# Two weight tiles on a second DMA queue, their high halves on the vector engine, and the first chunk's products in three passes

## The chip, the core and the metric

The kernel runs on one core of a Trainium2 chip. A core has five engines with an instruction queue each: TensorE (PE, the matrix products), VectorE (DVE), ScalarE (ACT), GpSimd (POOL) and SyncE (SP, which here only issues DMA transfers). The engines run side by side and wait for each other through semaphores. The metric is the device time of one execution in microseconds, lower is better.

## The reference, cut to what matters

```python
def reference(A_x, A_wqkv, A_wo, B_x, B_w1, B_b1, B_w2, gate_w):
    x = A_x                                          # (1, 2048, 640); B_x is not used
    g = sigmoid((x * gate_w).sum(-1, keepdims=True))
    a = A_ref(x, A_wqkv, A_wo)     # qkv = x @ wqkv; 32 heads of 20; softmax over 8 keys at distance 0, 2, ..., 14; @ wo
    b = B_ref(x, B_w1, B_b1, B_w2) # h = x @ w1 + b1 (640 -> 1728); h * tanh(softplus(h)); @ w2 (1728 -> 640)
    return g * a + (1 - g) * b
```

All of it is float32. Only the first product, x @ wqkv, is touched by the change, and of it only the first part.

## The kernel before

**Three products for one.** TensorE works on a rounded format (float32r). So every float32 operand is split into a high half (a copy into the rounded format) and a low half (operand minus high half), and every product is made of three: high x high, high x low, low x high (`mm3`, lines 347 to 351: L349, L350, L351). `split` (L312) makes the halves: the high one by ScalarE (L314), the low one by the vector engine, or by whichever of VectorE and GpSimd is free (L317). `load_pair` (L335) puts a load (`dma`, L322, issued by SP at L323) and a split together.

**Tiling.** The 640 input features are five chunks of 128 (`kc` 0 to 4). The 2,048 positions are four blocks of 512 (`tb`); a tile of x is one block and one chunk, 128 x 512. The tiles of wqkv, `WQ[hq, kc]`, are 128 x 498 for the first group of heads: q, k and v of eight heads, some columns of w1, and gate_w twice. They are named x0 to x4 and w0 to w4 here for `tb` 0 and `hq` 0, by chunk.

**The start.** Nine products of zeros warm TensorE up (L291). Then the first unit of `qkv` (L456, the case `u == 0`) goes chunk by chunk over four output banks, as the tiles come in: for every chunk four times `mm3`, 12 products. Bank i takes positions 128 i to 128 i + 127 of the block as its stationary operand, the weight tile is the moving one. The other four banks follow, each with all its chunks, and then the products of the first dense layer, `mlp1`. The attention of a unit (`attention`, L381) is the vector engine's, and begins when its q, k and v are out of the banks.

**What sets the order.** The program is written as a list of tasks (`add`, L74) with an engine, a duration, a rank, what they come after, and the buffers that they take. `Plan.run` (L90) plays them on a clock of its own and so fixes the order of the instructions in each engine's queue. It looks at the engines in the order PE, ACT, DVE, POOL, SP (`LAG`, L62); a free engine takes, of its tasks that are ready and whose buffers are free, the one of the lowest rank, then the earliest in the list. Buffers come from rings, and a task may take one only in the order in which they were asked for (`fits`, L105). The staging buffers of the loads go round three rings, three to each (`stages`, L325): x0 and w0 take the first two of `raw`; x1, w1 and x2 those of `hb`; w2, x3 and w3 those of `e`; x4 and w4 are on `raw` again. A task's result counts as there for tasks of other engines after a lag of 120 ns (ACT, DVE) or 1,900 ns (SP, behind the transfer itself), for tasks of its own engine after 40 ns. What the chip does with the order, it does by semaphores; the planner's clock is not the chip's.

The activation tables are loaded at L254, ahead of everything that is planned.

Of the kernel before, what the change touches and what calls it, by code (L numbers as in the profile page):

```python
# [59 lines left out]
class Plan:  # L60
# [29 lines left out]
    def run(self):  # L90
        ready = {e: [] for e in self.LAG}
        busy = dict.fromkeys(self.LAG, False)
        events, n, left, wire = [], 0, len(self.tasks), 0.0


        quiet, gate, last, shared, phase, begun = 0.0, None, None, [], "", False
        loud = sum(t.kind != "" for t in self.tasks)
        for i, t in enumerate(self.tasks):
            t.key = (t.rank, i)
            t.rdy = 0.0  # L100
            if not t.waits:
                (shared if t.both else ready[t.eng]).append(t)
        now = 0.0

        def fits(t):  # L105
            want = {}
            for b in t.take:
                want[b.ring] = want.get(b.ring, 0) + 1
                if b.ring.free < want[b.ring] or b.ring.line[b.ring.at + want[b.ring] - 1] is not b:
                    return False  # L110
            return True

        while left:
            again = True
            while again:
                again = False
                for e in self.LAG:
                    if busy[e]:
                        continue
                    fit = [t for t in ready[e] if fits(t)]  # L120
                    on = begun and loud
                    if e == "POOL":
                        fit += [t for t in shared if fits(t)]
                        if on:
                            fit = [t for t in fit if now + t.ns[0] <= quiet + 150 or t.rank < 0]
                    elif e == "DVE":
                        fit += [t for t in shared if fits(t) and (now - t.rdy > self.PATIENCE or phase != "qk" or not on)]
                    if not fit:
                        continue
                    t = min(fit, key=lambda t: t.key)  # L130
                    if t.both:
                        shared.remove(t)
                        t.eng = e
                    else:
                        ready[e].remove(t)
                    if type(t.ns) is tuple:
                        t.ns = t.ns[e == "DVE"]
                    for b in t.take:
                        b.ring.free -= 1
                        b.ring.at += 1  # L140
                        b.t = b.make()
                    t.start = now
                    ins = t.fn(e) if t.both else t.fn()
                    if e == "POOL" and on and quiet > now and gate and ins:
                        self.follow(ins, gate)
                    if e == "DVE":
                        if t.kind:
                            begun = True
                            loud -= 1
                            phase = t.kind[:2]  # L150
                        if t.kind == "qk":
                            quiet, gate = now + 5700, last
                        last = ins or last
                    busy[e] = again = True
                    heapq.heappush(events, (now + t.ns, n, "idle", e))
                    end = now + t.ns
                    if e == "SP":
                        wire = max(wire, end) + t.land
                        end = wire
                    heapq.heappush(events, (end + self.LAG[e], n + 1, "done", t))  # L160
                    if e != "SP":
                        heapq.heappush(events, (end + 40, n + 2, "own", t))
                    n += 3
            if not events:
                stuck = [(t.eng, t.rank, t.waits, getattr(t.fn, "__qualname__", "")) for e in ready for t in ready[e]]
                raise RuntimeError(f"nothing can go on at {now}, {left} left: {stuck[:20]}")
            now, _, what, x = heapq.heappop(events)
            if what == "idle":
                busy[x] = False
                continue  # L170
            if what == "done":
                left -= 1
                x.at = now
                for b in x.hold:
                    b.left -= 1
                    if not b.left:
                        b.ring.free += 1
            for t in x.then:

                if (t.eng == x.eng and x.eng != "SP") != (what == "own"):  # L180
                    continue
                t.waits -= 1
                if not t.waits:
                    t.why, t.rdy = x, now
                    (shared if t.both else ready[t.eng]).append(t)
        return now
# [3 lines left out]
def kernel(ctx: ExitStack, tc: tile.TileContext, x, wq, wo, w1, b1, w2, out):  # L190
# [42 lines left out]
    def act_ns(n):  # L233
        return 95 + 0.95 * n
# [10 lines left out]
    def mm_ns(n):  # L245
        return 13.5 + (n + 15) // 16 * 16 / 2.4
# [4 lines left out]

    A.preload_act_table_set("natural_log_exp_and_others")  # L254
    bias = keep.tile([128, FC + 1], F32)
    ln2 = keep.tile([128, 1], F32)
    cap = keep.tile([128, 1], F32)
# [51 lines left out]
    cg = add("POOL", 5000, consts_g, rank=-1)  # L309


    def split(raw, hi, lo, n, after, eng, hold, take=(), rank=SOON):  # L312

        a = add("ACT", act_ns(n), lambda: A.activation(hi(), raw(), AF.Copy), after, rank=rank, take=take, hold=hold)  # L314

        def low(e=eng):
            return (V if e == "DVE" else G).tensor_tensor(lo(), raw(), hi().bitcast(F32), op=OP.subtract)  # L317

        b = add(eng, either(eng, n), low, [a], rank=rank, hold=list(take) + list(hold))
        return [a, b]  # L320

    def dma(out_ap, in_ap, after=(), rank=0.0, take=(), hold=(), size=262144):  # L322
        return add("SP", 450, lambda: nc.sync.dma_start(out_ap(), in_ap()), after, rank=rank, take=take, hold=hold, size=size)  # L323

    stages = {"i": 0, "of": (raw_buf, raw_buf, raw_buf, lambda: h_buf("hb"), lambda: h_buf("hb"), lambda: h_buf("hb"),  # L325
# [6 lines left out]
        stages["i"] += 1  # L332
        return stages["of"][stages["i"] % len(stages["of"])]()

    def load_pair(src, eng, n=512, rank=SOON, drank=0.0, after=(), wide=False, home=None):  # L335
        raw, p = stage(wide), pair_buf() if home is None else fixed(home)
        d = dma(lambda: raw.t[:, :n], src, after, rank=drank, take=[raw], size=n * 512)
        p.ready = split(lambda: raw.t[:, :n], lambda: p.t[:, 0, :n], lambda: p.t[:, 1, :n], n, [d], eng, [raw], [p], rank)
        return p

    def load_w(src, n, eng, rank=NEXT, drank=0.0, after=()):
# [94 lines left out]
    def qkv_part(ps, P, hq, i, kc, n):  # L436
        xs = tuple(X[2 * P + i // 4, kc].t[:, j, (i % 4) * 128:(i % 4 + 1) * 128] for j in range(2))
        mm3(ps.t[:, :n], xs, tuple(WQ[hq, kc].t[:, j, :n] for j in range(2)), kc == 0, kc == KC - 1)

    def qkv_evac(u, P, hq, i, ps, done):  # L440
        kv, q, s = KV[UNIT[u]], Q[UNIT[u]], 4 * (1 - i // 4) + i % 4
        before = freed.get((u - 2, s), []) if u < 7 else [zero2[0]]
        a = add("ACT", 400, lambda: A.activation(kv[:, 7 + s], ps.t[:, QF:3 * QF].rearrange("p (a b) -> p a b", a=2), AF.Copy),  # L443
                [done] + before, rank=SOON, hold=[ps])
        b = add("ACT", 280, lambda: A.activation(q[:, s], ps.t[:, :QF], AF.Copy), [a], rank=SOON, hold=[ps])

        def rest():
            A.activation(hx[:, P, i, hq], ps.t[:, 3 * QF:3 * QF + RQ], AF.Copy)
            if hq == 0:
                z = ps.t[:, NCOL - 2:NCOL - 1]  # L450
                A.activation(zt[:, P, s:s + 1], z, AF.Exp, scale=-1.0)

        c = add("ACT", 170 * (2 if hq == 0 else 1), rest, [b], rank=SOON, hold=[ps])
        return a, b, c

    def qkv(u, P, hq):  # L456
# [3 lines left out]
        pss = [ps_buf() for _ in range(8)]  # L460
        if u == 0:
            last = warmed
            for kc in range(KC):
                for i in range(4):
                    last = pe_add(3 * mm_ns(n), lambda i=i, kc=kc: qkv_part(pss[i], P, hq, i, kc, n),
                               [last] + X[0, kc].ready + WQ[hq, kc].ready, take=[pss[i]] if kc == 0 else [],
                               hold=[pss[i], X[0, kc], WQ[hq, kc]])
                    if kc == KC - 1:
                        ev[i] = qkv_evac(u, P, hq, i, pss[i], last)
# [232 lines left out]
    def wq_in(hq, kc, eng, **k):  # L702
        n = NCOL if hq == 0 else NCOL - 2
        WQ[hq, kc] = load_pair(lambda: wq[hq, kc][:, :n], eng, n=n, wide=hq == 0, **k)
# [3 lines left out]

    for kc in range(KC):
        x_in(0, kc, "DVE", drank=-1.0)  # L710
        wq_in(0, kc, "DVE", drank=-1.0)
    bias_in = dma(lambda: bias, lambda: b1, rank=-0.5, size=7168)
    const_v = add("DVE", 400, consts_v, [bias_in], rank=NEXT)
    for kc in range(KC):
# [93 lines left out]
```

## Time and profile before

| What | Value |
|---|---|
| median of 3 runs | 657.4 us (657.2 to 657.87) |
| the profiled execution's own time | 657.01 us |
| its span, first to last instruction | 655.2 us |
| mean granted TensorE clock | 0.999 |
| TensorE busy | 648.8 us |
| VectorE busy | 558.7 us |
| ScalarE busy | 349.9 us |
| GpSimd busy | 61.6 us |

In a row of the timeline stand start and duration in us, the engine, the line of the kernel, the operation, the tile written and the tile read, and in brackets the idle time of the engine ahead of it and what ended it. SPq is SP's queue of DMA issues; the duration there is that of the issue and not of the transfer. A row of a view by stretch gives from and to, the length, then busy us and number of instructions for PE, PEld (weight loads of TensorE), DVE, ACT and POOL, then the granted TensorE clock, the share of time that the DMA engines were busy, and GB/s. A row of a view of DMA issues gives the tiles, the count, the size, and the us from issue to landing. Tiles of x for the first block go to a fixed place and are called kvq after their split; weight tiles are called pair.

### The profile page before, as it was taken

Reading aid. Unit: us, or ns where it says so; the run is one execution under the profiler, and the core shown is the slowest. Engines: PE = TensorE matmul, PEld = TensorE weight load, DVE = VectorE, ACT = ScalarE, POOL = GpSimd, SP = SyncE. Lnnn points to the kernel's source line nnn. Section 1 sums busy time; section 2 is a strip of 40 time slices with the busy share of each in tenths; the row PEclk is TensorE's granted clock in tenths of the full one; section 3 lists DMA queues with packets and bytes.
Section 4 is the critical chain, followed back from the end, with each engine's and each line's share of the span. In section 5 each row is a group of like instructions: output and inputs, shape, how many; then the busy total and the mean of one; then the engine's idle time right before and its main releaser. Section 6 shows DMA issues by size and latency. Waiting matters only on the chain.

```text
span 655.2 us, 8076 instructions
## 1 busy us (share of the span) xinstructions
PE 648.8 (99%) x2869; PEld 537.6 (82%) x2869; DVE 558.7 (85%) x495; ACT 349.9 (53%) x724; POOL 61.6 (9%) x41
## 2 busy tenths in 40 slices
PE   9999999999999999999999999999999999999997
PEld 6888888888888888888888887888888888888886
DVE  6599999999998998999899989999999999934311
ACT  6689469639928963982896275434423134313100
POOL 2121000000000000000100100036002400212000
PEclk9999999999999999999999999999999999999999
DMA  9763355322314431331234267825546226645322
GB/s 312 235 49 113 99 112 120 111 64 84 106 57 139 126 106 33 89 121 57 77 106 145 58 186 243 263 66 168 166 116 200 78 75 202 186 130 159 114 80 81
DMA packets 55017, 82.38 MB, mean 126 GB/s; under 512 B 8144, under 2 KB 23760, under 8 KB 54976
## 3 DMA queue, kind: packets, MB, share of 16 engines
q1 hardware_dynamic: 54976, 81.86, 42.6%
q8 instruction: 22, 0.36, 0.2%
q14 instruction: 19, 0.16, 0.1%
HBM read 44.94 MB, written 27.80 MB: 111 GB/s over the span
## 4 chain that ended last, share of the span: by engine, by line
PE 98%; DVE 1%; issue 0%; DMA 0%; ACT 0%; SPq 0%; DVEq 0%
PE bank L350 32%; PE bank L351 32%; PE bank L349 32%; PE bank L614 1%; PE bank L615 1%; DMA raw<-in_wq 0%; DVE pair L317 0%; DVE kvq L693 0%; ACT pair L314 0%; DVE pr L407 0%; SPq L323 0%; DVEq L317 0%
## 5 line engine op out<-in xcount | busy, mean ns | idle before, releaser
L350 PE MATMUL bank<-pair 128*128 128x512 f32 (+2 forms) x432 | 167.3, 387 | 1.3 <-DVE pair L317 1.3
L349 PE MATMUL bank<-pair 128*128 128x512 f32 (+2 forms) x432 | 167.0, 387 | 0.0
L351 PE MATMUL bank<-pair 128*128 128x512 f32 (+2 forms) x432 | 167.0, 387 | 0.0
L386 DVE TENSOR_TENSOR pr<-kvq 128x2560 f32<-128x2560 f32 x32 | 92.4, 2887 | 4.6 <-issue 4.1
L350 PEld LDWEIGHTS bank<-pair 128*128 128x128 f32 x432 | 81.1, 188 | 17.7 <-DVE pair L317 2.2
L349 PEld LDWEIGHTS bank<-pair 128*128 128x128 f32 x432 | 81.1, 188 | 16.5 <-ACT kvq L638 0.6
L351 PEld LDWEIGHTS bank<-pair 128*128 128x128 f32 x432 | 81.2, 188 | 15.5
L350 PE MATMUL bank<-pair,w 128*128 128x512 f32 x234 | 91.0, 389 | 0.0
L349 PE MATMUL bank<-pair,w 128*128 128x512 f32 x234 | 91.0, 389 | 0.0
L351 PE MATMUL bank<-pair,w 128*128 128x512 f32 x234 | 91.0, 389 | 0.0
L407 DVE TENSOR_TENSOR pr<-kvq,lg 128x2560 f32<-128x2560 f32 x32 | 90.1, 2817 | 0.7
L389 DVE TENSOR_REDUCE lg<-pr 128x128 f32<-128x2560 f32 x32 | 90.0, 2812 | 0.5
L443 ACT ACTIVATE kvq<-bank 128x320 f32<-128x320 f32 x64 | 27.9, 439 | 97.1 <-PE bank L351 96.5
L350 PE MATMUL bank<-pair,kvq 128*128 128x512 f32 (+2 forms) x196 | 75.8, 387 | 0.2 <-DVE pair L317 0.2
L351 PE MATMUL bank<-pair,kvq 128*128 128x512 f32 (+2 forms) x196 | 75.9, 387 | 0.0
L349 PE MATMUL bank<-pair,kvq 128*128 128x512 f32 (+2 forms) x196 | 75.8, 387 | 0.0
L349 PEld LDWEIGHTS bank<-pair,w 128*128 128x128 f32 x234 | 43.9, 188 | 9.2
L351 PEld LDWEIGHTS bank<-pair,w 128*128 128x128 f32 x234 | 43.9, 188 | 9.2
L350 PEld LDWEIGHTS bank<-pair,w 128*128 128x128 f32 x234 | 43.9, 188 | 9.1
L411 DVE TENSOR_TENSOR pr<-pr 128x1280 f32<-128x1280 f32 x32 | 48.8, 1525 | 0.3
L525 DVE SCALAR_TENSOR_TENSOR hb<-e,hb 128x512 f32<-128x512 f32 (+1 forms) x56 | 39.7, 710 | 10.3 <-ACT e L523 10.0
L314 ACT ACTIVATE pair<-raw 128x512 fp32r<-128x512 f32 (+2 forms) x53 | 32.9, 628 | 27.7 <-PE bank L351 16.9
(94 smaller groups left out, 893.4 us busy)
## 6 DMA issues: line engine op xcount, KB each, us to landing
act<-hb SPq DMA_DIRECT2D x52, 256.0 KB, 2.0
o<-ot SPq DMA_DIRECT2D x64, 80.0 KB, 1.9
raw<-act SPq DMA_DIRECT2D x20, 256.0 KB, 3.5
raw<-in_w SPq DMA_DIRECT2D x15, 320.0 KB, 3.0
kvq<-kvq SPq DMA_DIRECT2D x8, 560.0 KB, 4.1
e<-act SPq DMA_DIRECT2D x17, 256.0 KB, 2.8
hb<-act SPq DMA_DIRECT2D x15, 256.0 KB, 3.1
raw<-in_wq SPq DMA_DIRECT2D x15, 248.0 KB, 3.7
```

Source lines behind the costliest of these rows:

```text
L314: a = add("ACT", act_ns(n), lambda: A.activation(hi(), raw(), AF.Copy), after, rank=rank, take=take, hold=hold)
L349: nc.tensor.matmul(ps, ah, bh, start=first, stop=False)
L350: nc.tensor.matmul(ps, ah, bl, start=False, stop=False)
L351: nc.tensor.matmul(ps, al, bh, start=False, stop=last)
L386: return V.tensor_tensor(pr, window(kv, s0, 0), q[:, s0:s0 + 2, None, :].to_broadcast([128, 2, W, QF]), op=OP.mult)
L389: V.tensor_reduce(lg[:, s0:s0 + 2].rearrange("p s w h -> p (s w h)"), pr.rearrange("p s w (h d) -> p (s w h) d", d=DH), op=OP.add, axis=AX.X)
L407: V.tensor_tensor(pr.rearrange("p s w (h d) -> p s w h d", d=DH), vw, lg[:, s0:s0 + 2, :, :, None].to_broadcast([128, 2, W, HQ, DH]), op=O ...
L411: prev = add("DVE", 1510, lambda: V.tensor_tensor(pr[:, :, 0:4], pr[:, :, 0:4], pr[:, :, 4:8], op=OP.add), [prev], rank=r)
L443: a = add("ACT", 400, lambda: A.activation(kv[:, 7 + s], ps.t[:, QF:3 * QF].rearrange("p (a b) -> p a b", a=2), AF.Copy), [done] + before, ...
L525: v = add("DVE", 700, lambda: V.scalar_tensor_tensor(hb.t[:n], e.t[:n], -1.0, hb.t[:n], op0=OP.add, op1=OP.mult), [a], rank=NEXT, hold=[e, ...
L614: nc.tensor.matmul(pss[dc].t, wh, p.t[:, 0], start=False, stop=False)
L615: nc.tensor.matmul(pss[dc].t, wl, p.t[:, 0], start=False, stop=True)
```

## The change

Four things change. The loads of w0 and w1 become tasks of ACT's queue instead of SP's, with rank -3; the planner lets a transfer that is not SP's land 1,900 ns plus its size by 270 bytes per ns after its issue. The high halves of w0 and w1 become copies by the vector engine. The table load moves from ahead of the plan into it, as a task of ACT of rank -2. And chunk 0 of the first unit goes by pass over the four banks, high x high for all four, then high x low, then low x high, each pass a task that waits for its own halves, instead of bank by bank.

```diff
@@ -157,6 +157,8 @@
                     if e == "SP":
                         wire = max(wire, end) + t.land
                         end = wire
+                    else:
+                        end += t.land
                     heapq.heappush(events, (end + self.LAG[e], n + 1, "done", t))
@@ -251,7 +253,6 @@
-    A.preload_act_table_set("natural_log_exp_and_others")
     bias = keep.tile([128, FC + 1], F32)
@@ -309,9 +310,12 @@
-    def split(raw, hi, lo, n, after, eng, hold, take=(), rank=SOON):
-
-        a = add("ACT", act_ns(n), lambda: A.activation(hi(), raw(), AF.Copy), after, rank=rank, take=take, hold=hold)
+    def split(raw, hi, lo, n, after, eng, hold, take=(), rank=SOON, hi_eng="ACT"):
+
+        if hi_eng == "DVE":
+            a = add("DVE", 400, lambda: V.tensor_copy(hi(), raw()), after, rank=rank, take=take, hold=hold)
+        else:
+            a = add("ACT", act_ns(n), lambda: A.activation(hi(), raw(), AF.Copy), after, rank=rank, take=take, hold=hold)
@@ -319,7 +323,10 @@
-    def dma(out_ap, in_ap, after=(), rank=0.0, take=(), hold=(), size=262144):
+    def dma(out_ap, in_ap, after=(), rank=0.0, take=(), hold=(), size=262144, eng="SP"):
+        if eng == "ACT":
+
+            return add("ACT", 450, lambda: A.dma_start(out_ap(), in_ap()), after, rank=rank, take=take, hold=hold, size=1900 * 270 + size)
         return add("SP", 450, lambda: nc.sync.dma_start(out_ap(), in_ap()), after, rank=rank, take=take, hold=hold, size=size)
@@ -437,6 +444,12 @@
+    def qkv_pass(pss, a, b, n):
+
+        for i, ps in enumerate(pss):
+            nc.tensor.matmul(ps.t[:, :n], X[0, 0].t[:, a, i * 128:(i + 1) * 128], WQ[0, 0].t[:, b, :n],
+                             start=a == b, stop=False)
+
@@ -460,10 +473,15 @@
             last = warmed
-            for kc in range(KC):
+            xh, xl = X[0, 0].ready
+            wh, wl = WQ[0, 0].ready
+            for a, b, w in ((0, 0, [xh, wh]), (0, 1, [wl]), (1, 0, [xl])):
+                last = pe_add(4 * mm_ns(n), lambda a=a, b=b: qkv_pass(pss[:4], a, b, n), [last] + w, take=pss[:4] if a == b else [],
+                              hold=pss[:4] + [X[0, 0], WQ[0, 0]])
+            for kc in range(1, KC):
                 for i in range(4):
                     last = pe_add(3 * mm_ns(n), lambda i=i, kc=kc: qkv_part(pss[i], P, hq, i, kc, n),
-                               [last] + X[0, kc].ready + WQ[hq, kc].ready, take=[pss[i]] if kc == 0 else [],
+                               [last] + X[0, kc].ready + WQ[hq, kc].ready,
                                hold=[pss[i], X[0, kc], WQ[hq, kc]])
@@ -708,7 +726,9 @@
     for kc in range(KC):
         x_in(0, kc, "DVE", drank=-1.0)
-        wq_in(0, kc, "DVE", drank=-1.0)
+        wq_in(0, kc, "DVE", drank=-1.0 if kc > 1 else -3.0, **({"queue": "ACT", "hi_eng": "DVE"} if kc < 2 else {}))
+        if kc == 1:
+            add("ACT", 1300, lambda: A.preload_act_table_set("natural_log_exp_and_others"), rank=-2.0)
```

`load_pair` passes `queue` and `hi_eng` on to `dma` and `split`.

More of the change, by code (lines that the diff above doesn't have):

```diff
@@ L333, in stage, with load_pair @@
         return stages["of"][stages["i"] % len(stages["of"])]()
-    def load_pair(src, eng, n=512, rank=SOON, drank=0.0, after=(), wide=False, home=None):
+    def load_pair(src, eng, n=512, rank=SOON, drank=0.0, after=(), wide=False, home=None, queue="SP", hi_eng="ACT"):
         raw, p = stage(wide), pair_buf() if home is None else fixed(home)
-        d = dma(lambda: raw.t[:, :n], src, after, rank=drank, take=[raw], size=n * 512)
-        p.ready = split(lambda: raw.t[:, :n], lambda: p.t[:, 0, :n], lambda: p.t[:, 1, :n], n, [d], eng, [raw], [p], rank)
+        d = dma(lambda: raw.t[:, :n], src, after, rank=drank, take=[raw], size=n * 512, eng=queue)
+        p.ready = split(lambda: raw.t[:, :n], lambda: p.t[:, 0, :n], lambda: p.t[:, 1, :n], n, [d], eng, [raw], [p], rank, hi_eng)
         return p
```

## The prediction

> **What bounds the kernel now.** I read the page first: busy shares, then the chain that ended last.
>
> ```profile
> PE 648.8 (99%) x2869; PEld 537.6 (82%) x2869; DVE 558.7 (85%) x495; ACT 349.9 (53%) x724; POOL 61.6 (9%) x41
> PE 98%; DVE 1%; issue 0%; DMA 0%; ACT 0%; SPq 0%; DVEq 0%
> ```
>
> TensorE is busy for 648.8 of 655.2 us and carries 98% of the chain. So only its idle time can be won, and any idle time added to it is paid in full. Where the idle time lies is read from busy time by stretch (first PE figure: busy us).
>
> ```profile
> 82.00:164.00 82.00, 82.00 (x367) 68.57 (x366) 77.03 (x66) 59.20 (x121) 1.58 (x1) 1.00 0.40 98
> 164.00:400.00 236.00, 236.00 (x1061) 198.60 (x1060) 221.37 (x175) 158.22 (x344) 6.26 (x5) 1.00 0.35 106
> 400.00:410.00 10.00, 8.71 (x37) 6.50 (x36) 9.90 (x13) 6.18 (x11) 0.00 (x0) 1.00 0.74 214
> 410.00:650.00 240.00, 240.00 (x1060) 198.25 (x1059) 182.72 (x177) 67.88 (x113) 40.40 (x23) 1.00 0.46 139
> ```
>
> From 82 to 650 us TensorE stands still once, for 10.00 - 8.71 = 1.29 us near 403. The change works on the first 9 us. There the timeline of before (start, duration, engine, line) is, for the first tiles of x (x0, x1) and of the weights (w0, w1):
>
> ```profile
> 0.75 1.28 ACT L254 ACT_TABLE_LOAD   x1 [0.75 <-PEq L796]
> 0.75 0.38 SPq L323 DMA_DIRECT2D raw<-in_x  x1
> 0.87 0.27 DVE L287 MEMSET lg<- 128x256 uint32 x1 [0.87 <-PEq L796]
> 1.19 0.42 SPq L323 DMA_DIRECT2D raw<-in_wq  x1
> 1.20 3.93 PE L291 MATMUL bank<-lg 128*128 128x512 bf16 x9 [1.20 <-DVE lg L287]
> 1.65 0.43 SPq L323 DMA_DIRECT2D hb<-in_x  x1
> 3.52 0.63 ACT L314 ACTIVATE kvq<-raw 128x512 fp32r<-128x512 f32 x1 [1.49 <-DMA raw<-in_x]
> 4.18 0.69 DVE L317 TENSOR_TENSOR kvq<-raw,kvq 128x512 fp32r<-128x512 f32 x1 [3.04 <-ACT kvq L314]
> 4.20 0.62 ACT L314 ACTIVATE pair<-raw 128x498 fp32r<-128x498 f32 x1
> 4.86 0.68 DVE L317 TENSOR_TENSOR pair<-raw,pair 128x498 fp32r<-128x498 f32 x1
> 4.88 0.49 PE L349 MATMUL bank<-pair,kvq 128*128 128x498 f32 x1
> 5.59 0.49 PE L350 MATMUL bank<-pair,kvq 128*128 128x498 f32 x1 [0.22 <-DVE pair L317]
> 6.24 0.63 ACT L314 ACTIVATE kvq<-hb 128x512 fp32r<-128x512 f32 x1 [1.42 <-DMA hb<-in_x]
> 6.90 0.69 DVE L317 TENSOR_TENSOR kvq<-hb,kvq 128x512 fp32r<-128x512 f32 x1 [1.37 <-ACT kvq L314]
> 7.55 0.68 DVE L317 TENSOR_TENSOR pair<-hb,pair 128x498 fp32r<-128x498 f32 x1
> 7.96 0.39 PE L351 MATMUL bank<-pair,kvq 128*128 128x498 f32 x1
> 8.19 0.38 PE L349 MATMUL bank<-pair,kvq 128*128 128x498 f32 x1
> ```
>
> The first real product starts at 4.88, when w0's high half is there; the second waits for w0's low half (4.86 + 0.68 = 5.54) until 5.59; the second chunk starts at 8.19. From 5.59 to 8.19 lie the 11 other products of chunk 0, 2.60 us, and the last two starts are 0.23 apart.
>
> The landings, issue to last byte (last column, us):
>
> ```profile
> raw<-in_x SPq DMA_DIRECT2D x1, 256.0 KB, 2.7
> raw<-in_wq SPq DMA_DIRECT2D x1, 249.0 KB, 3.0
> hb<-in_x SPq DMA_DIRECT2D x1, 256.0 KB, 4.6
> hb<-in_wq SPq DMA_DIRECT2D x1, 249.0 KB, 4.8
> ```
>
> The SP queue's issues stand about 0.47 apart (1.19, 1.65), so w1 goes out near 2.12. x0 lands at 3.5, w0 at 4.2, x1 at 6.2, w1 at 6.9. ScalarE stood idle for x1 until 6.24. So the transfers do not land at an even pace: x1 comes 2.0 us behind w0, w1 0.7 behind x1.
>
> **The change part by part.** *The issues.* The planner walks its engines in the order PE, ACT, DVE, POOL, SP, and a load may start only when its staging buffer is next in its ring. At time 0 the raw ring's next buffer belongs to x0, which SP has not taken yet, and the hb ring's to x1. So neither weight load fits, and ACT takes the only task that does: the table load, whatever the ranks say. ACT's queue becomes table load, w0, w1; SP's becomes x0, x1, w2, x3, x2, w3, x4. The planner's clock is used here for order alone.
>
> When ACT's queue gets to w0 no row shows: it is bounded by the start of the load (0.75) and the first thing ACT is seen to do after it (3.52). Before, w0 went out at 1.19. I take the load's end, 0.75 + 1.28 = 2.03, the row in between. The two issues (0.42 to 0.43 each on SP) end by 2.9, inside ACT's idle 1.49 us before 3.52, so they cost nothing; were that cover gone, x0's high half would be late by as much. SP loses two issues, so x1 goes out at 1.19, in w0's old place.
>
> *The landing of x1, L.* Low end: w0's old landing, 4.20. High end: x1's row, 6.24. Between them lies x0's 3.52 plus two transfers at 0.68 (6.24 to 6.92), 4.88. The same three transfers, x0, x1 and w0, have to come through before x1 and w0 are both complete, and in the trace the third came at 6.24; so I go nearer to that row and take L = 5.7, for w0 likewise.
>
> The Trainium skill, "DMA: Bandwidth & Descriptors" (section "Issuing engines are not separate DMA queues"), says that transfers issued from different engines run on the same 16 DMA engines and interleave, and that several issuers save only issue time. This speaks against the change, and by it w0 gains nothing from a queue of its own; by "a second queue is a second path" w0 and x1 would both be in by 4.9. No run of before has two queues, so the trace does not decide.
>
> *The vector engine.* It now makes w0's and w1's high halves. A copy of that shape is in no row: at least 0.27 (a memset of half as many elements), at most 0.69 (two inputs, same size); I take 0.5, twice the memset. By the planner's own figures it runs x0's low half to 4710 ns, w0's high half from 4714 to 5114, and then w0's low half becomes eligible at 5154, while x1's low half has been so since 4993. So x1's low half goes in first. The order is x0 low, w0 high, x1 low, w0 low, w1 high, w2 low, w1 low. That is the wait the change adds: w0's low half, which every product of the second pass needs, stands behind x1's landing, x1's high half on ScalarE and x1's low half.
>
> Priced with the rows of before: from ScalarE's start on x1 (6.24) to the end of the second low half (7.55 + 0.68 = 8.23) pass 1.99 us. So w0's low half ends at L + 1.99, against 5.54 before. w0's high half (5.7 + 0.5 = 6.2) is done before x1's low half may start (5.7 + 0.66), so it costs nothing; a landing of w0 over 0.16 us after x1's would show.
>
> *Pass by pass.* The same 12 products, each with its own weight load as before. The four high-high ones run while the low half is awaited, three more than before: 3 x 0.23 = 0.69 us won. After w0's low half come 8 products: 2.60 - 0.69 = 1.91. Chunk 1 starts at L + 1.99 + 0.05 + 1.91 = L + 3.95, against 8.19: the delay is L - 4.24. With L = 5.7: +1.5 us. With 6.24: +2.0. With 4.88: +0.6. With 4.20 the vector engine binds instead: x0 low until 4.87, w0 high until 5.37, then 0.65 (6.90 to 7.55) and 0.68, so 6.70, and 6.70 - 5.54 - 0.69 = +0.5. No value of L makes it a gain.
>
> *What comes next.* w1's low half ends 0.5 + 0.65 + 0.68 = 1.8 us after w0's; TensorE wants it 0.05 + 1.91 + 0.23 = 2.2 after, so it is just covered, if w2 is in. Two ScalarE copies go (0.62 each), the vector engine gains two of 0.5: hidden in its waits (3.04, 1.37). x2 goes out behind x3, and w4 behind three loads that it led; each is wanted by its own chunk, one every 2.7 us (12 x 0.23) from 8.19 on: x2 at 10.9, w4 at 16.4. w4's row of before:
>
> ```profile
> 6.96 0.33 SPq L323 DMA_DIRECT2D raw<-in_wq  x1
> raw<-in_wq SPq DMA_DIRECT2D x1, 249.0 KB, 4.7
> ```
>
> It landed at 11.7, so three loads of 0.7 to 0.9 us ahead of it are covered by 4.7 us. x2 lands as the seventh transfer, about 3 us after x1; its low half ends well before chunk 2, which is late by the same delay.
>
> *To the end.* The first attention follows TensorE:
>
> ```profile
> 33.40 2.83 DVE L386 TENSOR_TENSOR pr<-kvq 128x2560 f32<-128x2560 f32 x1 [4.10 <-issue]
> ```
>
> The vector engine idles 4.10 us before it, so it starts later by the same amount, and TensorE has no idle time until 403 that could take up a delay. In the planner's books chunk 1 begins 0.14 us earlier than before, a uniform shift once the first loads are used up, so I expect the later order to stay.
>
> Sum: the profiled run took 657.01 us (span 655.2); +1.5 gives 658.5. The median of the runs shown is 657.4, so 658.9.
>
> **The rivals.** *1, the queues help (not slower).* ACT's queue passes the table load at once and the slow landing of x1 was SP's backlog: L between 4.2 and 4.9, +0.5 to +0.65, about 658.0, no measurable change. For it: the later transfers land 0.7 apart. Against it: x1's row, 6.24. It decides below L = 5.5, where the delay is under 1.3.
>
> *2, the table load holds ACT's queue.* w0 goes out near 3.4 and lands 3.0 to 4.6 later (both rows above), at 7.2 in the middle; high half to 7.7, x1 low 0.65, low half 0.68, so 9.0: 9.0 - 5.54 - 0.69 = +2.8, 660.2. For it: no ACT row between 2.03 and 3.52.
> The Trainium skill, "ScalarE: Activation LUTs" (section "What ACT_TABLE_LOAD costs"), adds to about 1283 ns of load some 1380 ns of drain. The load's row agrees (1.28); no row shows the drain.
>
> *3, the clock falls.* The granted clock (third column from the right) at the end of the trace:
>
> ```profile
> 650.00:653.40 3.40, 1.47 (x7) 0.89 (x5) 1.37 (x2) 0.00 (x0) 0.00 (x0) 1.00 0.30 111
> 653.50:655.20 1.70, 0.00 (x0) 0.00 (x0) 0.00 (x0) 0.00 (x0) 0.00 (x0) 0.50 0.17 64
> ```
>
> After 3.4 us with 1.47 busy it is half. Between the warm-up's end (5.13) and 7.7 TensorE would now do four products, about 1.2 us; a stretch of 3.4 us around that holds 1.2 + 0.8 = 2.0, not far off. Half the clock for 3.4 us costs 1.7: 657.4 + 1.5 + 1.7 = 660.6.
> The Trainium skill, "TensorE: Matmul & The Clock Gate" (Part 1), has the clock gated again after an idle window of about 3.4 us; the two rows agree, and by it gaps of 1.2 us each are too short.
>
> *4, the planned order shifts later on*, and with it the stall at 403:
>
> ```profile
> 403.52 0.50 PE L350 MATMUL bank<-pair 128*128 128x512 f32 x1 [1.08 <-DVE pair L317]
> 407.46 0.50 PE L350 MATMUL bank<-pair 128*128 128x512 f32 x1 [0.20 <-DVE pair L317]
> ```
>
> TensorE waits there for low halves queued behind attention steps. If they go first it saves up to 1.3: 657.6, and less with a small L; one more step of 2.83 ahead of them would cost that much. Against it: the uniform shift.
>
> **How the numbers follow.** What tells from no change here is about 0.2%, 1.3 us. Forecast 0.47, of which 0.12 with L under 5.5 stays inside that bound; rival 1 0.17; rival 2 0.10; rival 3 0.14; rival 4 0.12 (0.05 faster, 0.04 same, 0.03 slower). Slower 0.35 + 0.10 + 0.14 + 0.03 = 0.62, same 0.12 + 0.17 + 0.04 = 0.33, faster 0.05. The likeliest case's own range is 658.2 (L 5.0) to 659.4 (6.24). The whole range, 657.7 to 660.6, takes in rivals 1 and 2 and reaches to 3.
>
> **What would show it.** Right: on ACT the table load ahead of two issues; on the vector engine x1's low half ahead of w0's; four high-high products, a wait for a low half, then eight; chunk 1 starting 0.6 to 2.0 later than 8.19; the same shift at 33.40 and at the end. Wrong: w0's low half before 6.2, products over 0.4 us apart after 8, or another stall than the one near 403.

## The result, and the profile after

| What | Before | After |
|---|---|---|
| median of 20 executions each | 657.22 us | 657.95 us |
| lowest and highest | 656.84 to 657.87 | 657.66 to 659.6 |
| the profiled execution's own time | 657.01 us | 659.59 us |
| its span | 655.2 us | 657.8 us |

The ratio is 1.0015, with a 95% interval of 1.0009 to 1.0022. The kernel became slower, by 0.7 us of median (0.6 to 1.4 by the interval). That is real, but inside the 0.2%, 1.3 us, that the prediction took as the bound of "no change".

The 20 executions of the change fall into two groups: 16 lie at 657.66 to 658.64, four at 659.19 to 659.6. The profiled execution belongs to the upper group, so its 2.58 us over before have to be taken apart into what the change always costs and what only some executions pay.

The start comes first. In the timeline of the changed kernel, the rows of before have these counterparts (L316 is the vector engine's copy, L318 ScalarE's, L321 the low half, L450 the product by passes, L356 to L358 the three products of `mm3`):

```profile
0.74 1.28 ACT L731 ACT_TABLE_LOAD   x1 [0.74 <-PEq L816]
...
0.77 0.39 ACTq L329 DMA_DIRECT2D raw<-in_wq  x1
1.19 0.42 SPq L330 DMA_DIRECT2D hb<-in_x  x1
1.19 0.46 ACTq L329 DMA_DIRECT2D hb<-in_wq  x1
...
4.99 0.51 DVE L316 CAST pair<-raw 128x498 fp32r<-128x498 f32 x1
...
5.07 0.63 ACT L318 ACTIVATE kvq<-hb 128x512 fp32r<-128x512 f32 x1 [0.72 <-DMA hb<-in_x]
...
5.65 3.50 PE L450 MATMUL bank<-pair,kvq 128*128 128x498 f32 x12 [0.43 <-DVE pair L316]
5.73 0.69 DVE L321 TENSOR_TENSOR kvq<-hb,kvq 128x512 fp32r<-128x512 f32 x1 [0.23 <-ACT kvq L318]
...
6.34 0.67 DVE L321 TENSOR_TENSOR pair<-raw,pair 128x498 fp32r<-128x498 f32 x1
...
6.93 0.41 DVE L316 CAST pair<-hb 128x498 fp32r<-128x498 f32 x1
...
8.99 0.39 PE L356 MATMUL bank<-pair,kvq 128*128 128x498 f32 x1
```

TensorE's loads of the stationary operand (PEld), one to each product, show the three parts of chunk 0 that the prediction had named, four high-high products, a wait for w0's low half, then eight:

```profile
5.62 1.25 PEld L450 LDWEIGHTS bank<-pair,kvq 128*128 128x128 f32 x4 [1.31 <-issue]
7.07 1.65 PEld L450 LDWEIGHTS bank<-pair,kvq 128*128 128x128 f32 x8 [0.20 <-DVE pair L321]
```

One load takes 0.19, so the first four stand about 0.35 apart and the eight about 0.21. In this execution TensorE's full clock came only during the first four (the trace has it from 6.75 on), and these filled nearly the whole wait: 0.20 of it is left.

The vector engine makes x1's low half (5.73) ahead of w0's (6.34), as the prediction had read it out of the planner's figures. w0's low half is there at 6.34 + 0.67 = 7.01, not at 5.54. The second chunk starts at 8.99 instead of 8.19, 0.80 late. The first attention of the same execution carries that on, 34.19 against 33.40:

```profile
34.19 2.83 DVE L393 TENSOR_TENSOR pr<-kvq 128x2560 f32<-128x2560 f32 x1 [1.54 <-ACT kvq L456]
```

The rest of the 2.58 us lies near 403. First the product of before that stands just ahead of its second stall there, then TensorE after:

```profile
406.87 0.39 PE L349 MATMUL bank<-pair 128*128 128x512 f32 x1
```

```profile
403.59 0.50 PE L356 MATMUL bank<-pair 128*128 128x512 f32 x1 [0.65 <-ACT pair L318]
405.03 0.50 PE L357 MATMUL bank<-pair 128*128 128x512 f32 x1 [0.94 <-DVE pair L321]
...
406.08 0.59 PE L358 MATMUL bank<-pair 128*128 128x512 f32 x1
...
409.46 0.43 PE L357 MATMUL bank<-pair,w 128*128 128x512 f32 x1
```

And the stretches around it (from and to, length, busy us of PE, PEld, DVE, ACT and POOL, the granted clock third from the right):

```profile
402.70:406.10 3.40, 1.82 (x8) 1.06 (x7) 3.33 (x6) 2.47 (x5) 0.00 (x0) 1.00 0.47 132
406.10:409.50 3.40, 3.40 (x10) 2.62 (x9) 3.40 (x4) 3.07 (x6) 0.00 (x0) 0.50 0.80 208
```

The product after the long wait is the one of 403.52 before; it now starts at 405.03, 1.51 late, of which 0.8 were there from the start. Here TensorE waited for ScalarE's high half and then for the low half. After that the granted clock is 0.50 for one stretch of 3.4 us: the eight products from 406.08 to 409.46 take 3.38 us, 0.42 each, instead of 8 x 0.23 = 1.84, 1.5 lost. Before's second stall (406.87 to 407.46, 0.36 more than one product) vanishes in it. 1.51 + 1.54 - 0.36 = 2.7 by these rows, 2.6 by the two spans. So of the profiled difference 0.8 us is the change's own, and the larger part is a longer stall and a fall of the clock in this execution. Why ScalarE's high half was late there is not shown.

The queues behind the start are the same. Taken engine by engine from the two traces, with line and buffer numbers left out, the instructions are identical to the end on ScalarE, the vector engine, GpSimd and SP after the first 61, 26, 11 and 36 of the changed kernel's, and TensorE's do not differ by these names, which do not tell chunk 0's halves apart.

### The profile page after: what moved, and what is told of

It reads as the page before. It is cut to its first block, busy times and chain, and to the rows that moved or that the text cites. A ratio compares the mean times of both kernels' runs of the same rounds, so it can differ in the third digit from the quotient of the medians.

```text
span 657.8 us, 8075 instructions
## 1 busy us (share of the span) xinstructions
PE 650.8 (99%) x2869; PEld 539.2 (82%) x2869; DVE 558.0 (85%) x497; ACT 347.9 (53%) x722; POOL 59.8 (9%) x41
## 4 chain that ended last, share of the span: by engine, by line
PE 97%; DMA 1%; DVE 1%; ACT 0%; issue 0%; DVEq 0%
PE bank L358 32%; PE bank L357 32%; PE bank L356 32%; DMA raw<-in_w 1%; PE bank L632 1%; PE bank L633 1%; PE bank L450 1%; DMA raw<-in_x 0%; DVE pair L321 0%; DVE pr L418 0%; DVE kvq L711 0%; DVE pr L419 0%; DVE kvq L321 0%; ACT pair L318 0%; ACT kvq L318 0%
## 5 line engine op out<-in xcount | busy, mean ns | idle before, releaser
L356 PE MATMUL bank<-pair 128*128 128x512 f32 (+2 forms) x432 | 167.6, 388 | 0.6 <-ACT pair L318 0.6
L358 PE MATMUL bank<-pair 128*128 128x512 f32 (+2 forms) x432 | 167.7, 388 | 0.0
L356 PEld LDWEIGHTS bank<-pair 128*128 128x128 f32 x432 | 81.4, 188 | 17.3 <-ACT pair L318 1.1
L358 PEld LDWEIGHTS bank<-pair 128*128 128x128 f32 x432 | 81.5, 189 | 15.7
L356 PE MATMUL bank<-pair,w 128*128 128x512 f32 x234 | 91.3, 390 | 0.0
L358 PE MATMUL bank<-pair,w 128*128 128x512 f32 x234 | 91.0, 389 | 0.0
L358 PE MATMUL bank<-pair,kvq 128*128 128x512 f32 (+2 forms) x192 | 74.3, 387 | 0.0
L356 PE MATMUL bank<-pair,kvq 128*128 128x512 f32 (+2 forms) x192 | 74.2, 386 | 0.0
L357 PE MATMUL bank<-pair,kvq 128*128 128x512 f32 (+2 forms) x192 | 74.2, 386 | 0.0
L356 PEld LDWEIGHTS bank<-pair,w 128*128 128x128 f32 x234 | 44.1, 188 | 9.1
L358 PEld LDWEIGHTS bank<-pair,w 128*128 128x128 f32 x234 | 44.0, 188 | 9.3
L318 ACT ACTIVATE pair<-raw 128x512 fp32r<-128x512 f32 (+2 forms) x52 | 32.3, 628 | 29.7 <-PE bank L358 16.6
```

Of the source, the lines that this page charges most:

```text
L356: nc.tensor.matmul(ps, ah, bh, start=first, stop=False)
L357: nc.tensor.matmul(ps, ah, bl, start=False, stop=False)
L358: nc.tensor.matmul(ps, al, bh, start=False, stop=last)
```

## The experiments

Each line of a short diff below is against the changed kernel, unless it says otherwise. The theory after the result: the change delays chunk 1 by "landing of x1 minus 4.24", because x1's low half stands ahead of w0's; the passes give back 0.69. The rivals were a cost of the second queue itself, of the vector engine's copies, and of the clock.

### Chunk 0 bank by bank again

```diff
-            xh, xl = X[0, 0].ready
-            wh, wl = WQ[0, 0].ready
-            for a, b, w in ((0, 0, [xh, wh]), (0, 1, [wl]), (1, 0, [xl])):
...
-            for kc in range(1, KC):
+            for kc in range(KC):
```

> Chunk 0 goes bank by bank again; everything else as changed. If the place of w0's low half in the vector engine's queue sets the start, and the passes only fill the wait for it, the second product waits until about 7.05, 11 products follow it, and chunk 1 starts at 7.05 + 2.6 = 9.65: 0.66 later than with the passes (8.99), 1.4 us slower than before. If the passes do not matter (TensorE would be held by the tiles of chunk 1 anyway): no different from the changed kernel, 0.7 slower than before.

Measured: 659.56 us, 1.0029 [1.0018, 1.004]. The lowest three of seven executions took 658.47 to 658.68, some 0.8 above the bulk of the change and 1.3 to 1.5 above before, where 1.4 was expected; the others reach to 661.35. In the profiled one the second product waits for w0's low half, as foreseen, and then the clock falls:

```profile
5.68 0.47 PE L356 MATMUL bank<-pair,kvq 128*128 128x498 f32 x1 [0.81 <-ACT kvq L318]
7.04 0.49 PE L357 MATMUL bank<-pair,kvq 128*128 128x498 f32 x1 [0.90 <-DVE pair L321]
...
8.67 0.62 PE L356 MATMUL bank<-pair,kvq 128*128 128x498 f32 x1
9.08 0.62 PE L357 MATMUL bank<-pair,kvq 128*128 128x498 f32 x1
```

```profile
4.40:7.80 3.40, 1.70 (x6) 0.86 (x5) 2.73 (x5) 0.63 (x1) 0.78 (x3) 1.00 0.97 344
7.90:11.20 3.30, 3.30 (x10) 2.63 (x9) 2.51 (x5) 2.69 (x5) 0.00 (x0) 0.50 1.05 382
```

So the passes are worth about what they were priced at, 0.69, where w0's low half is late. They may do one thing more that the price left out: three more products in the wait keep TensorE busier. With 1.70 us of 3.4 busy, the clock was halved for the next 3.4 us: that is the prediction's rival of the clock, at the place where it had looked for it, though in a kernel with less work there than the change has. One such fall in 657 us leaves a mean granted clock of 0.997 (1.7 of 657 lost). Three of the seven executions here have 0.996 or 0.997; two of the change's 20 do.

The Trainium skill, "TensorE: Matmul & The Clock Gate" (section "Part 1: The HAM clock gate"), describes a free-running window of about 3.4 us and a half clock after an idle one. The length agrees with these rows (3.4 us at 0.50); but none of the two gaps here was longer than 0.90 us, so a stretch half idle in pieces was enough, and the measurement decides.

### w0's low half directly behind its high half

In `split`, for w0 alone, both halves become one task of the vector engine:

```diff
+        if hi_eng == "BOTH":
+            def halves():
+                V.tensor_copy(hi(), raw())
+                return V.tensor_tensor(lo(), raw(), hi().bitcast(F32), op=OP.subtract)
+            a = add("DVE", 400 + dve_ns(n), halves, after, rank=rank, take=take, hold=hold)
+            return [a, a]
```

> w0's high and low half are one task, so that x1's low half no longer stands between them; everything else as changed. If the order is the cause, w0's low half ends near 6.1 instead of 7.01, the 12 products of chunk 0 run without a wait from 5.6, and chunk 1 could start at 8.4; there w1's low half (about 8.85, behind x3's) holds its second product, against 9.21 with the change. So 0.3 faster than the changed kernel, 0.4 slower than before. If contention by the second queue is the cause: no different from the changed kernel.

Measured: 658.19 us, 1.0019 [1.001, 1.0028], in two groups again: six executions at 657.48 to 658.19, five at 659.28 to 659.57. Most of the lower group lies where the expectation had put the kernel, 0.4 above before; the upper group it had not foreseen. The same kernel was run once more, to see whether the groups come back:

> The kernel with w0's two halves in one task, 9 warm-up products, again and beside the one with 10. Two groups again, at 657.6 and at 659.4, some 4 in 10 in the upper one; if the profiled execution falls into the upper one, its products of chunk 0 and 1 stand 0.42 apart until a release of the clock near 7 or later, and the other groups' does not.

Measured: 658.33 us, 1.0019 [1.001, 1.0028], seven at 657.68 to 658.37 and four at 659.09 to 659.66. TensorE in the profile of the first run, from the lower group:

```profile
5.68 2.96 PE L457 MATMUL bank<-pair,kvq 128*128 128x498 f32 x12 [0.93 <-ACT kvq L325]
8.48 0.39 PE L363 MATMUL bank<-pair,kvq 128*128 128x498 f32 x1
8.90 0.49 PE L364 MATMUL bank<-pair,kvq 128*128 128x498 f32 x1
```

Now chunk 0 runs without a wait, and chunk 1 starts at 8.48. But its second product then stands till 8.90 for w1's low half (before, it started at 8.41, 0.23 behind the first). So of 0.80 us about a third came back, not all: behind w0's the next low half is late. The median is no better than the change's, since nine of its 22 executions in the two runs lie in the upper group.

### The change, with the table load ahead of the plan again

```diff
+    A.preload_act_table_set("natural_log_exp_and_others")
     bias = keep.tile([128, FC + 1], F32)
...
-        if kc == 1:
-            add("ACT", 1300, lambda: A.preload_act_table_set("natural_log_exp_and_others"), rank=-2.0)
```

> The change with one thing undone: the table load is ahead of the plan again, so that in the planner's books w0 and w1 land 1.3 us earlier. On the vector engine both halves of w0 then go first, but x2's low half goes ahead of w1's. If the order in the queues is the cause of the loss, chunk 0 runs from 5.0 without a wait, and chunk 1 is held by w1's low half, near 8.2, about as before the change: 657.0 to 657.3, 0.6 to 0.9 faster than the change. If the second queue or the high halves on the vector engine cost by themselves: 0.5 or more slower than before.

Measured: 657.14 us, 1.0002 [0.9993, 1.001]. All of the loss is gone, and all 11 executions lie within 657.06 to 657.65, below the lowest of the change's 20 (657.66). ACT's queue, the copies and the passes are as in the change; on the chip the table load runs at the same time, 0.74 to 2.02. What differs is the planner's clock: without the 1.3 us booked on ACT, w0 is there earlier in its books, and it puts w0's low half first. (The order moves elsewhere too: x0's low half goes behind w0's, and SP sends x2 ahead of w2.)

```profile
4.08 0.80 DVE L317 CAST pair<-raw 128x498 fp32r<-128x498 f32 x1 [2.94 <-DMA raw<-in_wq]
4.91 0.68 DVE L322 TENSOR_TENSOR pair<-raw,pair 128x498 fp32r<-128x498 f32 x1
```

```profile
5.02 2.96 PE L451 MATMUL bank<-pair,kvq 128*128 128x498 f32 x12
7.82 0.39 PE L357 MATMUL bank<-pair,kvq 128*128 128x498 f32 x1
8.39 0.49 PE L358 MATMUL bank<-pair,kvq 128*128 128x498 f32 x1 [0.18 <-DVE pair L322]
```

This settles the cause of the loss as far as the order goes: with the second queue and the copies kept no loss shows (657.14 against 657.1, though the interval reaches to 0.1%), so the planner's order made it. That the place of w0's low half is what counts in that order is read from the timelines, where the formula gives chunk 1's start. The queue and the copies are not free, though. x0 landed at 3.81, where before had 3.52, and w0's copy took 0.80; the first product starts at 5.02 instead of 4.88, and the passes cover that. The run also shows why nothing is won. Chunk 1 starts 0.37 earlier than before, and its second product, which waits for w1's low half, starts at 8.39 against 8.41.

### The passes alone, on the kernel before

```diff
+            for a, b, w in ((0, 0, [xh, wh]), (0, 1, [wl]), (1, 0, [xl])):
...
-            for kc in range(KC):
+            for kc in range(1, KC):
```

> Before, with nothing but chunk 0 pass by pass. The three products pulled into the wait are 0.69 us, but chunk 1 then waits for its own tiles: w1's high half is there at 7.52 and its low half at 8.23 as before, so the second product of chunk 1 starts at 8.26 instead of 8.41 and the gain is 0.1 to 0.2 us (657.0). If the tiles of chunk 1 were no limit: 0.7 faster (656.4).

Measured: 657.04 us, 0.9998 [0.9989, 1.0007].

```profile
4.96 2.99 PE L442 MATMUL bank<-pair,kvq 128*128 128x498 f32 x12
7.87 0.50 PE L349 MATMUL bank<-pair,kvq 128*128 128x498 f32 x1
8.59 0.50 PE L350 MATMUL bank<-pair,kvq 128*128 128x498 f32 x1 [0.22 <-DVE pair L317]
```

Chunk 0 ends 0.3 us earlier and chunk 1 stands for its low half: on one queue x1 landed at 6.53 in this execution, and the vector engine was done with w1's low half at 8.5. The passes shorten what the supply of the next chunk then takes back.

### One weight tile on ACT's queue

Two kernels that tried to beat both: the table load ahead of the plan, the passes kept, and only w0 on ACT's queue; in the first w0's high half is the vector engine's, in the second ScalarE's.

```diff
+    A.preload_act_table_set("natural_log_exp_and_others")
...
+        wq_in(0, kc, "DVE", drank=-1.0 if kc else -3.0, **({} if kc else {"queue": "ACT", "hi_eng": "DVE"}))
```

> w0 alone on ACT's queue, its high half by the vector engine, the passes kept, the table load ahead of the plan as before. In the planner's books w0 then lands before x0's high half is made, so both halves of w0 go ahead of x0's and x1's low halves. With w0 in at 4.0: high half to 4.5, low half to 5.2, x0's low half to 5.8, products from 4.55, chunk 1 at 4.55 + 0.33 + 11 x 0.23 = 7.4, so 0.7 to 0.8 faster than before (656.5). If the order is not the cause: like the changed kernel, 0.7 slower than before. If the clock is still at half for the first products: 0.3 to 0.6 less gain.

> w0 alone on ACT's queue, its high half by ScalarE as before, the table load ahead of the plan as before, the passes kept. x1 no longer stands ahead of w0 on either engine. If the order in the queues is the cause, TensorE starts at 5.05, chunk 1 at 5.05 + 0.33 + 11 x 0.23 = 7.9, so 0.3 faster than before (656.9). If a second DMA queue costs something by itself (x0 landed 0.2 later): 0.2 to 0.8 slower than before.

Measured: 657.24 us, 1.0000 [0.9991, 1.0009], with w0's high half on the vector engine; 657.02 us, 0.9998 [0.9989, 1.0006], with it on ScalarE. Neither can be told from before. The small gain expected of the second lies inside its interval; that of the first, 0.75, lies outside. But the eleven executions of the first are not alike. Four took 656.64 to 656.68, less than any of the 29 of before beside them (lowest 656.86), six 657.22 to 657.53, and one, with a mean granted clock of 0.997, took 659.18. Its expectation had named the reason for 0.3 to 0.6 less gain, the clock still at half for the first products. The profiled execution, 657.31, shows it: no product waits, and yet chunk 1 starts at 8.48, where 5.02 + 12 x 0.23 = 7.8 was to be had:

```profile
5.02 3.63 PE L451 MATMUL bank<-pair,kvq 128*128 128x498 f32 x12
8.48 0.39 PE L357 MATMUL bank<-pair,kvq 128*128 128x498 f32 x1
```

```profile
4.90:6.50 1.60, 1.60 (x5) 1.26 (x5) 1.59 (x3) 1.11 (x3) 0.76 (x2) 1.00 1.03 388
6.50:8.50 2.00, 2.00 (x11) 1.66 (x10) 2.00 (x4) 1.86 (x4) 0.00 (x0) 1.00 1.04 382
```

Up to 6.5 us five products, the last of the warm-up among them, take 1.60 us, about half the pace of the eleven in the 2.00 us behind them: TensorE's full clock came late in this execution. That the four fast executions had it early is not shown; none of them was profiled. In the second kernel ScalarE began x0's high half only at 4.09, when x0 landed, later than in any other profile here, and made w0's behind it, so that the products start at 5.29, not at 4.9. Why x0 was so late is open: with two queues it landed at 3.72 to 3.99 in the other profiles, with one at 3.51 or 3.52.

### How long TensorE is warmed up

Three runs on the upper group. The change with ten products of zeros in place of nine, the kernel of w0's low half with ten, and before with six.

```diff
-WARM = 9
+WARM = 10
```

(In before it is 6 in place of 9.)

> The changed kernel with 10 warm-up products instead of 9, which fills the idle time from 5.2 to 5.65. If the executions above 659 us come from a clock that is released one window (3.4 us) later or falls back because TensorE stood idle there, they become fewer, and the rest stays at 657.7 to 658.2. If they come from elsewhere (the stall near 403, the transfers): 1 in 5 as before. Chunk 1 still starts at 9.0 in either case.

> The kernel with w0's two halves in one task, with 10 warm-up products instead of 9. With 9 it had 5 of 11 executions at 659.3 to 659.6 and the rest at 657.5 to 658.2. If those five come from the idle time between the warm-up's end and the first product (up to 5.65), the upper group goes, and the median falls to 657.6. If not, about as many stay above 659.

> Before, with 6 warm-up products instead of 9: TensorE then stands idle from 3.8 to 4.9, and nothing else changes. If an idle gap ahead of the first chunk is what exposes a run to a late or lost clock, a part of the executions is 1 to 1.7 us slower than before and the others equal to it. If the gap is harmless: no execution above 658.3.

Measured: 658.0 us, 1.0013 [1.0004, 1.0022], for the change with ten; 658.29 us, 1.0014 [1.0005, 1.0023], for the other with ten; 658.71 us, 1.0026 [1.0015, 1.0037], for before with six.

With ten, none of 22 executions lies above 659 us; with nine, 13 of 42 do (4 of 20 of the change, 9 of 22 of the other). So the upper group goes with the length of the warm-up. The second expectation missed in its median, 657.6. Five of the eleven executions lie at 658.45 to 658.79, above all seven of the lower group with nine (657.68 to 658.37), so not all of the loss went. In the one of them that was profiled x3 landed late, at 7.79, and chunk 1's second product, whose low half stands behind x3's, stood till 9.79; whether the other four lost their time in the same way was not seen.

The change with ten also gives a profile with no fall of the clock, and so the change's own cost by itself:

The first row is ScalarE's on x1, those behind it TensorE's.

```profile
5.34 0.63 ACT L318 ACTIVATE kvq<-hb 128x512 fp32r<-128x512 f32 x1 [0.72 <-DMA hb<-in_x]
```

```profile
5.92 1.15 PE L450 MATMUL bank<-pair,kvq 128*128 128x498 f32 x4 [0.69 <-DVE pair L316]
7.34 2.08 PE L450 MATMUL bank<-pair,kvq 128*128 128x498 f32 x8 [0.28 <-DVE pair L321]
9.26 0.39 PE L356 MATMUL bank<-pair,kvq 128*128 128x498 f32 x1
...
404.59 0.50 PE L357 MATMUL bank<-pair 128*128 128x512 f32 x1 [1.15 <-DVE pair L321]
408.53 0.50 PE L357 MATMUL bank<-pair 128*128 128x512 f32 x1 [0.24 <-DVE pair L321]
```

x1 came at 5.34, so the formula says +1.10. Chunk 1 is 1.07 late (9.26 against 8.19), the two stalls near 403 are 1.07 late and as long as before (1.15 and 0.24 against 1.08 and 0.20), and this execution's 658.07 is 1.06 over the profiled 657.01 of before. The delay goes from the start to the end undiminished. Here the four high-high products run at the full clock and end well ahead of w0's low half, and yet chunk 1 starts where the formula says: in these two profiles a late clock cost nothing at the start, since the four products fitted into the wait.

Before with six shows the other side. Its warm-up ends at 3.94, TensorE stands still for 0.88 us, and the first chunk runs at half pace to its end (0.41 from 9.87 to 10.28, then 0.22 from 10.61 to 10.83):

```profile
4.82 0.78 PE L349 MATMUL bank<-pair,kvq 128*128 128x498 f32 x1 [0.88 <-ACT pair L314]
...
9.87 0.62 PE L351 MATMUL bank<-pair,kvq 128*128 128x498 f32 x1
10.28 0.49 PE L349 MATMUL bank<-pair,kvq 128*128 128x498 f32 x1
10.61 0.38 PE L350 MATMUL bank<-pair,kvq 128*128 128x498 f32 x1
10.83 0.39 PE L351 MATMUL bank<-pair,kvq 128*128 128x498 f32 x1
```

Every one of its executions took 658.19 or more. That was expected of some of them only.

## Why the prediction was right, and where its size was off

It said slower by 1.5 us, 658.9, own range 658.2 to 659.4. The median is 657.95, inside the whole range (657.7 to 660.6) and below the own one: the direction and the mechanism held, the size came out at half. A delay under 1.3 us it had called no measurable change, and given that 0.33, against 0.62 for a larger loss. So the range held because it took in rival 1, whose price of 658.0 is nearer to the result than the forecast is.

**The orders: right.** ACT's queue is table load, w0, w1. The vector engine's is x0 low, w0 high, x1 low, w0 low, w1 high. One detail behind that was wrong: between w1's high and low half stands x3's low half, not w2's. It cost nothing in the change.

**The formula: right.** "L - 4.24" with the measured L of 5.07 gives +0.83, measured +0.80; with 5.34 it gives +1.10, measured +1.07. The terms behind it held: the copy took 0.51 (taken 0.5), and the passes gave back about 0.69 by the first experiment.

**The landing of x1: the term that failed.** L was taken as 5.7, nearer to before's 6.24, on the ground that three transfers have to come in either way. It was 5.07 in the profile, and 4.71 to 5.34 in seven other profiles with two queues. With one queue it was 5.65 (before with six warm-up products), 6.24 and 6.53. The 5.07 lies just above the upper end of rival 1, "the queues help", whose price of 0.5 to 0.65 for L up to 4.9 is close to the lower group's 0.7. What speaks for rival 1 in the trace is the rate of the transfers over the first 9 us, in 40 slices, before and then after:

```profile
GB/s 0 0 0 0 0 0 0 36 164 91 146 355 407 383 390 329 190 209 246 262 198 178 222 277 325 361 377 358 376 369 278 305 387 388 431 393 394 404 406 380
```

```profile
GB/s 0 0 0 0 0 0 0 27 255 280 297 324 368 410 384 390 416 387 357 338 381 363 372 384 352 336 364 410 391 353 359 347 347 377 382 377 323 318 386 410
```

With one queue the rate sinks to about 200 GB/s from 3.6 to 5.2 us, while x1 is on its way; with two there is no such dip. The prediction had weighed a rule of the Trainium skill here, "DMA: Bandwidth & Descriptors" (section "Issuing engines are not separate DMA queues"), by which another issuer saves only issue time. In these two profiles more than that was saved: four tiles were issued by 1.65 in place of 2.55, 0.9 us, and x1 came 1.2 us earlier, though it was issued only 0.46 earlier. Between the nearest two profiles, 5.34 and 5.65, it is only 0.3, and x0 came later with two queues (3.72 to 4.09) than with one (3.51 or 3.52). Why the third transfer of one queue is slow was not settled.

**The issue of w0: wrong, at no cost.** It was taken to leave at 2.03, behind the table load; it left at 0.77, 0.03 us after the load began. Rival 2, that the load holds the queue, falls with it. So w0 did not land at 5.7 either, as x1 was taken to, but near 4.0 (3.2 us after its issue). That cost and won nothing, as the vector engine was on x0's low half until about 5.0.

**The later order: right.** The queues are the same, and the delay of the start arrives at the end (34.19 against 33.40; 1.07 near 403 and 1.06 at the end with ten warm-up products). Of rival 4 the part with another order falls. Its stall near 403 is there in all profiles. In the change's it was 0.7 us longer, and with chunk 0 bank by bank TensorE also waited twice there, 0.58 and 1.04.

**The clock, rival 3: a real mechanism, with the wrong weight and place.** It was priced as one case, +1.7 at the start in every execution. It came in some executions. In the profiled one it cost 1.5 us near 403, after 3.4 us with 1.82 busy. With chunk 0 bank by bank it came at the start. Products over 0.4 us apart after 8 without a wait between them, one of the prediction's own signs of being wrong, are there in the profiled execution near 406, and are not in the one with ten warm-up products. The prediction also read the last two rows of before as agreeing with an idle window; the first of them has 1.47 us busy of 3.40.

What the upper executions without a profile lost was not seen, but their mean granted clocks tell something. Of the change's four, two have 0.997, the profiled one and that at 659.5, which one fall leaves. The other two, and all nine of the kernel with w0's low half directly behind, have 1.00: no such fall. A late release, the change from half to full clock, would not show in that column (see the last section), and that ten warm-up products remove the group speaks for it; no profile caught one there.

## What to carry to other kernels

Where a planner's clock orders the queues, a duration that is booked on an engine can cost through the order alone: here 1.3 us of table load, which the chip ran beside everything else, put one low half behind another, and with the load out of the plan the loss was gone. When a wait is shortened, look at once at the next item of the same supply: chunk 1's low half gave back what chunk 0 won in several of these kernels. And a kernel that lives on one engine should be priced with that engine's clock in mind: fill waits near the warm-up with products, and read executions one by one, since an effect that comes in a fifth of them hides in a median and can fill a profile.

## What the runs showed of the hardware

- The clock fell after stretches of 3.4 us with 1.70 and 1.82 us busy in several pieces. It did not fall after one with 2.43, the change's start with ten warm-up products:

```profile
4.70:8.10 3.40, 2.43 (x10) 1.38 (x9) 2.97 (x6) 1.58 (x3) 0.74 (x1) 1.00 1.03 373
```

But it did not fall either after one with 1.73, from 650.4 to 653.8 in the second run of w0's low half directly behind its high half: the granted clock is 1.00 there and in the 2.0 us behind it. So the busy time of a stretch, as the profile has it, does not alone tell when the clock falls.

- In the traces the times at full clock are whole multiples of 3.413 us: 399.36 in the changed kernel's (117 times), 648.53 in before's (190 times). The first release, the change from half to full clock, lay at 4.14 to 6.75 us in the nine profiles with nine warm-up products. So how a wait near 403 falls on these stretches differs from one execution to the next, which fits a fall in some of them only.
- Before the first release, the profile's clock column reads 1.00 while products run at half pace: with six warm-up products the stretch below has ten instructions where before's has 17 (the count behind the first busy time).

```profile
7.10:10.50 3.40, 3.40 (x10) 2.74 (x9) 3.00 (x5) 2.85 (x5) 0.00 (x0) 1.00 1.03 377
```

- With six warm-up products and 0.88 us of idle time behind them, the full clock came at about 10.5 us, in before's profile at about 4.9.
- Issues of transfers behind a table load on ACT's queue go out at once (0.77, while the load runs from 0.74 to 2.02).
- The vector engine's copy of 128 x 498 took 0.51 and 0.41 us after 4.9 us, but 0.80 at 4.08, while GpSimd's memset ran (0.74 to 4.59). That the memset is the cause was not tested.
